# Projecting with the output weights held and h streamed: a GFNet mixing and SwiGLU kernel on one core

## The chip, the core and the metric

The kernel runs on one core of a Trainium2 chip. The metric is device time in microseconds (us) of one execution. TensorE (PE) multiplies matrices and loads the stationary operand with a separate instruction (PEld in the profile); VectorE (DVE), ScalarE (ACT) and GpSimd (POOL) work on elements; SyncE (SP) does no arithmetic here, it issues DMAs. SP and ACT issue DMAs on hardware queues (q1 and q10 in the profile), POOL on a software queue (q0). All queues are served by the same 16 DMA engines. Each engine works through its own instructions in order.

## The reference

`x` has 8 sequences of 3008 tokens with 256 channels, all float32. The first half is a filter in the frequency domain along the sequence, the second half a gated feed-forward layer with 1536 hidden units:

```python
X = np.fft.rfft(x, axis=1)
F = (filt_r + 1j * filt_i)[None, :, :]
y = np.fft.irfft(X * F, n=x.shape[1], axis=1)
g = y @ w_gate
silu = g * (1.0 / (1.0 + np.exp(-g)))
out = (silu * (y @ w_val)) @ w_out
```

## The kernel before

The transform is done by matmuls in stages ("pa", "pb", "pc", "pd" in the profile). The last stage, `stage3`, leaves the mixed tokens transposed, channels on partitions, in a tile `y` of eight parts (L774 to L791).

The feed-forward layer runs over 8 batches, 4 chunks each (752 tokens: two halves i of TH = 376 columns) and 3 groups g of hidden units, so 96 steps; batch 0 goes through its first three chunks group by group and parks partial outputs in `o_dram`. A step has 26 small matrix products (L860; tokens PQABE of the list below) which together give the hidden activations h of its group, as in a fast (Karatsuba- and Strassen-like) scheme with fewer products. ACT and DVE form sums in PSUM and SBUF between them. h stands in two tiles of seven parts, 128 x 376 each; POOL forms four of the combined parts (tokens S).

The projection follows one step later. It is a Strassen-Winograd form with seven products W1 to W7 per step (L932 to L943). Each takes two blocks of hidden units (`JB` = 2) and three windows of 128 tokens, `TOK = (0, 128, 248)`. For each window h is the stationary operand (128 x 128) and 128 columns of `wo_t` are streamed. Three windows of 128 cover 376 tokens, so eight are computed twice. A float32 matmul appears as two MATMUL records in the profile, so a W is 12 records. Results stand tokens on partitions, channels along the row, and after each product an "o" token adds the PSUM bank into the output tile in SBUF (L944 to L952; a copy by ACT for the first one of a chunk).

Stores: tokens x0.o to x5.o (L920 to L931) write the two output tiles `o0`, `o1`, three windows each, from POOL's queue: one DMA per window, 128 rows of 1 KB, six per chunk and only after its last group.

The order of all engines' work is written out by hand in `SCHEDULE` (L88): one step's tokens in order, where a prime means "of the step before last" (the projection's late part), and "t" tokens advance the transform of the next batch. `pin` keeps every engine's instructions in that order. `LAST` (L99) is what is left after the final step. The 26 weight tiles of a group do not fit twice: they are reloaded in place in four pieces (`PIECES`, L407, on SP), each as soon as its last product of the step is done, so that a piece issued after Q2 must be there when the next step opens with Q0.

Of the kernel before, what the change touches and what calls it, by code (L numbers as in the profile page):

```python
# [41 lines left out]
FP32 = mybir.dt.float32  # L42
# [6 lines left out]
B, S, C = 8, 3008, 256  # L49
# [6 lines left out]
NR = 2 * N1  # L56
NK = 4 * NS

NH = 4
NW = 2 * NH  # L60
NCHUNK = 32 // NW
TH = NH * NR
TOK = (0, 128, TH - 128)
NT = 3
NG = 3
JB = NJ // NG
# [11 lines left out]
WO = {1: 0, 7: 1, 2: 2, 3: 3, 5: 4, 6: 5, 4: 6}  # L78
HID = {1: 0, 6: 6, 4: 2, 2: 3, 5: 4, 7: 1, 3: 5}
# [6 lines left out]


SCHEDULE = """  # L88
Q0 o3' t4.2' W2 f0 S00' S01' x0.o' t0.0 x1.o' Q1 t0.1 x2.o' P3 x3.o' f1 t4.3' W1 x4.o' S10' x03 S11'
s13 x5.o' P1 o1 t0.2 P0 o2 c1 D01 A13 g1 c0 S20' Q2 S21' g0 y01 m13 t1.0 h0 f2 s01 W6 t1.1 h1 x23  # L90
D02 P2 o6 D12 A01 c2 B13 g2 n3' m01 t0.3 S30' t1.2 x02 W7 S31' g13 y12 y02 B01 h13 o7 t1.3 t2.0 s02
s12 g01 h2 Q3 t2.1 h01 e12 A02 y23 W4 e02 y03 m02 g3 A12 o4 t2.2 E12 m12 B02 t2.3 l12 E02 u12 e13
g02 t3.0 h3 s23 l02 B12 v12 E13 t3.1 h02 u02 A23 n2 l13 g12 v02 W5 s03 e23 h12 e01 m23 A03 o5 u13
E23 t3.2 m03 v13 E01 l23 e03 t3.3 t4.0 l01 u23 B23 v23 u01 t4.1 E03 n1 v01 g23 B03 l03 W3 h23 g03
u03 h03 v03
""".split()
KS = (-1, 0, 1, 2)

LAST = """  # L99
S00 S01 S10 S11 W1 o1 W2 o2 S20 S21 S30 S31 W6 o6 W5 o5 W3 o3 x0.o x1.o x2.o W7 o7 W4 o4 x3.o x4.o  # L100
x5.o
""".split()
BLOCKS = (0, 1, 3, 2)
PAIRS = ((0, 1), (1, 2), (2, 3), (0, 2), (1, 3), (0, 3))
# [68 lines left out]
def kernel(  # L173
# [10 lines left out]
    nc = tc.nc  # L184
# [18 lines left out]
    wdpool = pool("wdram", 1, DRAM)  # L203
# [24 lines left out]
                  for i in range(4)]  # L228
    yt_dram = [wdpool.tile([128, 3 * len(PAIRS), TQ], FP32, name=f"yt_{k}") for k in range(NT)]
    y_dram = [wdpool.tile([128, 8, TQ], FP32, name=f"y_{k}") for k in range(NCHUNK)]  # L230
    o_dram = [wdpool.tile([2, 128, len(TOK), C], FP32, name=f"o_{k}") for k in range(NT)]
    w_dram = wdpool.tile([NG, 128, NPR, 2, 128], FP32, name="w_all")
    wo_t = cpool.tile([128, NJ, 7, 128], FP32)

# [18 lines left out]
    pin = tc.keep_in_program_order  # L253

    def add(eng, dst, a, b):
        return eng.tensor_tensor(out=dst, in0=a, in1=b, op=ALU.add)  # L256
# [246 lines left out]
    def bank(name):  # L503
        return wps.tile([128, 512], FP32, name=f"w{name}", tag="w")
# [10 lines left out]
    class Spectral:  # L515
# [231 lines left out]
        def stage3(self, k, step):  # L747

            if step == 0:
                self.y[k] = ypool.tile([128, 8, TQ], FP32, name=f"y_{self.b}_{k}", tag="y")  # L750
            i, cb = divmod(step, 2)
            ps = (self.bank if k == 0 else fbank)(f"pd_{self.b}_{k}_{step}")
            psv = ps.rearrange("p a b -> p (a b)")[:, 0:TH].rearrange("p (n r) -> p n r", n=NH)
            flat = ps.rearrange("p a b -> p (a b)")
            back = self.b
            for j in range(len(BACK) if back else 0):
                first = BACK_AT[j]
                cols = back_t[0][:, first:first + N1 * len(BACK[j])]

                if j == 1:  # L760
                    rows = flat[:, 1:2 * 187 + 1].rearrange("p (z y) -> p z y", z=2)[:, :, ::2]
                else:
                    at = j // 2 * (2 * N1 + 1)
                    rows = flat[:, at:at + 6 * N1 - 1:2]
                pin(nc.tensor.matmul(out=rows, lhsT=self.t4[k, i][:, j, ts(cb, 128)], rhs=cols,  # L765
                                     start=j == 0, stop=True, skip_group_check=True))
            for n in range(0 if back else NH):
                pin(nc.tensor.matmul(out=psv[:, n, :],  # L768
                                             lhsT=self.t4[k, i][0:NK, n, ts(cb, 128)],
                                             rhs=wi_t, start=n == 0, stop=True,  # L770
                                             skip_group_check=True))
            yield

            y = self.y[k]  # L774

            def tokens(part, parts):
                return y[:, part:part + parts].rearrange("p t (r n) -> p n (t r)", n=NH)

            if cb == 0:
                pin(nc.scalar.copy(out=tokens(2 * i, 2), in_=psv))  # L780
                return
            for t in range(2):
                a, c = 2 * i + t, psv[:, :, ts(t, N1)]
                b, v, k = tokens(a, 1), tokens(4 + a, 1), KS[a]
                if k == 0:
                    pin(nc.scalar.copy(out=v, in_=c))
                elif k == -1:
                    pin(add(nc.vector, v, c, b))
                else:
                    pin(nc.vector.scalar_tensor_tensor(  # L790
                        out=v, in0=b, scalar=-float(k), in1=c, op0=ALU.mult, op1=ALU.add))  # L791
# [22 lines left out]
    outs = {}  # L814

    def takes_turns(b, k):
        return b == 0 and k < NT

    def new_outs(b, k, g):
        outs[b, k] = [opool.tile([128, len(TOK), C], FP32, name=f"o{i}_{b}_{k}_{g}",  # L820
                                 tag=f"o{i}", bufs=2) for i in range(2)]
        if g:
            for i in range(2):
                pin(nc.sync.dma_start(out=outs[b, k][i], in_=o_dram[k][i]))

    class Group:

# [19 lines left out]
        def bank(self, key, n=2):  # L847
            t = bank(f"{key}_{self.name}")
            self.tiles[key] = t[:, 0:2 * TQ].rearrange("p (z n) -> p z n", z=2) if n == 2 else \
                t[:, 0:384].rearrange("p (t c) -> p t c", c=128)  # L850
            return self.tiles[key]

        def product(self, p, key, start):
# [9 lines left out]
        def step(self, op, eng=None):  # L863
# [48 lines left out]
            elif kind == "n":  # L912
                if self.following:
                    self.following(i)

        def project(self, op, last=False):

            b, k, q = self.b, self.k, self.g
            kind, p = op[0], int(op[1])
            if kind == "x":  # L920
                i, t = divmod(p, len(TOK))
                if q < NG - 1 and takes_turns(b, k) and t == len(TOK) - 1:
                    pin(nc.sync.dma_start(out=o_dram[k][i], in_=outs[b, k][i]))
                if q == NG - 1:
                    skip = TOK[1] + 128 - TOK[2] if t == 2 else 0
                    rows = out[b * S:(b + 1) * S].rearrange("(r n) c -> r n c", n=32)
                    queue = (nc.sync, nc.scalar)[(p + i) % 2] if last else nc.gpsimd
                    pin(queue.dma_start(
                        out=rows[(TOK[t] + skip) // NH:(TOK[t] + 128) // NH, ts(2 * k + i, NH), :],
                        in_=outs[b, k][i][skip:128, t, :]))  # L930
                return  # L931
            at = {1: "A", 6: "A", 7: "A", 4: "A", 2: "F", 5: "G", 3: "G"}[p]  # L932
            if kind == "W":
                start = p in (1, 2, 5)
                if start:
                    self.bank(at, 3)
                for t, t0 in enumerate(TOK):
                    for i in range(JB):
                        pin(nc.tensor.matmul(  # L939
                            out=self.tiles[at][:, t, :], lhsT=self.hs[i][:, HID[p], t0:t0 + 128],  # L940
                            rhs=wo_t[:, JB * q + i, WO[p], :], start=start and t == 0 and i == 0,
                            stop=True, skip_group_check=True))
                return  # L943
            if q == 0 and p == 1:  # L944
                new_outs(b, k, q)
            i, cb = {1: (0, 0), 2: (0, 0), 6: (0, 1), 3: (0, 1), 4: (1, 0), 7: (1, 1),
                     5: (1, 1)}[p]
            dst = outs[b, k][i][:, :, ts(cb, 128)]
            if q == 0 and at == "A":
                pin(nc.scalar.copy(out=dst, in_=self.tiles[at]))  # L950
            else:
                pin(add(nc.vector, dst, dst, self.tiles[at]))  # L952

# [6 lines left out]
    x0 = [t[0:NR, 8 * C * i:8 * C * i + 8 * C] for t, i in ((wo_f, 0), (wo_f, 1), (y_f, 0))]  # L960
    x0 = [t.rearrange("p (n c) -> p n c", c=C) for t in x0]
# [6 lines left out]
    with tc.tile_pool(name="start", bufs=1) as spool0:  # L968
# [3 lines left out]
        f0 = spool0.tile([128, NS, C], FP32, name="f0")  # L972
# [8 lines left out]
        n = 0  # L981
# [68 lines left out]
        for p in ("A13", "A01"):  # L1050
            at = SLOT[p]
# [25 lines left out]
    opool = pool("op", 1)  # L1077
# [57 lines left out]
    for b in range(B):  # L1135
# [36 lines left out]
        for step in range(NCHUNK * NG + (b == B - 1)):  # L1172
            ghost = step == NCHUNK * NG
            k, g = order_of(b)[min(step, NCHUNK * NG - 1)]
# [13 lines left out]
            last = ghost or b == B - 1 and step == NCHUNK * NG - 1  # L1188
            for place, token in enumerate(SCHEDULE):
# [5 lines left out]
                if op[0] == "t":  # L1195
                    n = int(op[1])
# [64 lines left out]
```

## Time and profile before

| what | value |
|---|---|
| median of 7 runs | 2924.79 us (2922.44 to 2929.59) |
| the profiled execution's own time | 2922.45 us |
| its span in the profile | 2920.7 us |
| PE busy | 2887.8 us (99%) |
| DVE busy | 2031.3 us (70%) |
| ACT busy | 1599.7 us (55%) |
| POOL busy | 1595.3 us (55%) |
| granted TensorE clock | 0.998 |

The span is the time from the first to the last instruction; the profiled execution's own time is 1.75 us longer. "Busy" of PE counts overlapping matmuls once and says nothing of how fast they go, so the pace has to be taken from where one run of matmuls starts and the next one starts.

### The profile page before, as it was taken

How to read it: one execution, taken by the hardware profiler on the slowest of the kernel's cores; microseconds unless marked ns; L12 is line 12 of the kernel's file. 1: busy time of each engine (PE TensorE's matmuls, PEld its weight loads, DVE VectorE, ACT ScalarE, POOL GpSimd, SP SyncE). 2: the span in 40 equal slices, each digit the busy share in tenths (PEclk: the TensorE clock that was granted, in tenths of full speed). 3: DMA queues.
4: the chain of work that ended last, by engine and by line, in shares of the span. 5: the costliest groups of instructions: out<-in, count | busy, mean ns of one | idle time of the engine just before them, and what ended most of it. 6: DMA issues, size and time to landing. Idle time of an engine off the chain costs nothing.

```text
span 2920.7 us, 57842 instructions
## 1 busy us (share of the span) xinstructions
PE 2887.8 (99%) x20160; PEld 2830.7 (97%) x20160; DVE 2031.3 (70%) x4536; ACT 1599.7 (55%) x4190; POOL 1595.3 (55%) x1767
## 2 busy tenths in 40 slices
PE   8999999999999999999999999999999999999999
PEld 6889999999999999999999999999999999999999
DVE  6888766676676676767767667676666766666665
ACT  6775455545555555555455555555555555555554
POOL 4876655556454655455554556454565555555453
PEclk9999999999999999999999999999999999999999
DMA  8687865575565655656656566556565566644432
GB/s 229 211 261 249 301 195 188 175 228 180 181 193 181 223 182 175 198 174 211 207 165 203 175 199 213 172 185 194 191 206 179 175 204 196 206 134 159 145 129 88
DMA packets 234325, 559.55 MB, mean 192 GB/s; under 512 B 31757, under 2 KB 128015, under 8 KB 234035
## 3 DMA queue, kind: packets, MB, share of 16 engines
q1 hardware_dynamic: 199169, 486.24, 52.2%
q10 hardware_dynamic: 25938, 45.72, 4.6%
q0 software_dynamic: 8928, 23.89, 2.3%
q8 instruction: 162, 2.65, 0.4%
q14 instruction: 128, 1.05, 0.1%
HBM read 460.38 MB, written 95.34 MB: 190 GB/s over the span
## 4 chain that ended last, share of the span: by engine, by line
PE 93%; DMA 2%; DVE 1%; POOL 1%; issue 0%; SPq 0%; ACT 0%; DVEq 0%; POOLq 0%
PE wa L860 24%; PE wA L939 17%; PE wk L860 16%; PE we L860 12%; PE wG L939 8%; PE wF L939 4%; PE pd L765 3%; PE pc L731 2%; PE pb L698 2%; PE pa L639 1%; PE pa L641 1%; DMA lent<-later_tbl 1%; DMA lent<-d 0%; PE pa L658 0%; PE pd L768 0%
## 5 line engine op out<-in xcount | busy, mean ns | idle before, releaser
L860 PE MATMUL wa<-y_t,wt_t 128*128 128x188 f32 x4464 | 878.8, 323 | 3.8 <-issue 1.4
L860 PEld LDWEIGHTS wa<-y_t,wt_t 128*128 128x128 f32 x4464 | 729.7, 190 | 11.4 <-issue 3.8
L256 POOL TENSOR_TENSOR h<-h 128x376 f32<-128x376 f32 x190 | 182.9, 984 | 766.0 <-DVE h L907 766.0
L939 PE MATMUL wA<-wo_t,h 128*128 128x128 f32 x4608 | 576.9, 275 | 2.6 <-DVE o L256 2.1
L939 PEld LDWEIGHTS wA<-wo_t,h 128*128 128x128 f32 x4608 | 563.0, 192 | 8.6 <-DVE o L256 1.8
L860 PE MATMUL wk<-y,wt_t 128*128 128x188 f32 x2976 | 566.2, 323 | 0.0
L259 POOL TENSOR_TENSOR h<-h 128x376 f32<-128x376 f32 x570 | 562.8, 1009 | 0.5
L860 PEld LDWEIGHTS wk<-y,wt_t 128*128 128x128 f32 x2976 | 479.2, 190 | 7.1 <-DVE y L256 0.6
L860 PE MATMUL we<-y_t,wt_t 128*128 128x188 f32 x2232 | 431.5, 323 | 1.4 <-ACT we L891 1.4
L259 DVE TENSOR_TENSOR we<-we,m 128x376 f32<-128x376 f32 x576 | 317.0, 555 | 161.2 <-PE we L860 110.2
L860 PEld LDWEIGHTS we<-y_t,wt_t 128*128 128x128 f32 x2232 | 369.4, 190 | 1.8 <-ACT we L891 1.7
L259 POOL TENSOR_TENSOR D<-f,f 128x376 f32<-128x376 f32 x288 | 281.5, 991 | 93.8 <-ACT f L875 92.6
L263 DVE SCALAR_TENSOR_TENSOR y<-wk,c 128x376 f32<-128x376 f32 x480 | 244.7, 542 | 107.8 <-ACT we L891 52.1
L895 ACT COPY m<-wa 128x376 f32<-128x376 f32 x576 | 271.8, 472 | 85.2 <-PE wa L860 84.1
L939 PE MATMUL wG<-wo_t,h 128*128 128x128 f32 x2304 | 288.3, 275 | 0.6 <-DVE o L256 0.6
L902 ACT ACTIVATE u<-we 128x188 f32<-128x188 f32 x576 | 188.9, 328 | 179.5 <-DVE we L259 161.2
L902 ACT ACTIVATE g<-wa 128x188 f32<-128x188 f32 x576 | 187.3, 326 | 173.9 <-PE wa L860 166.4
L939 PEld LDWEIGHTS wG<-wo_t,h 128*128 128x128 f32 x2304 | 281.4, 192 | 0.8 <-DVE o L256 0.8
L875 ACT ACTIVATE f<-wk 128x376 f32<-128x376 f32 x288 | 139.3, 484 | 230.6 <-PE wk L860 221.2
L879 ACT COPY c<-wk 128x376 f32<-128x376 f32 x288 | 136.0, 472 | 224.9 <-PE wk L860 224.9
L882 DVE SCALAR_TENSOR_TENSOR x<-wk,f 128x376 f32<-128x376 f32 x192 | 104.3, 543 | 218.4 <-PE wk L860 216.7
L891 ACT COPY we<-y 128x376 f32<-128x376 f32 x480 | 224.3, 486 | 36.0 <-DVE h L907 16.6
(155 smaller groups left out, 4033.8 us busy)
## 6 DMA issues: line engine op xcount, KB each, us to landing
wt_t<-w_all SPq DMA_DIRECT2D x174, 896.0 KB
wt_t<-w_all SPq DMA_DIRECT2D x174, 768.0 KB
lent<-later_tbl SPq DMA_DIRECT2D x84, 256.0 KB
lent<-in_filt_r_dram SPq DMA_DIRECT2D x336, 64.0 KB
d<-lent ACTq DMA_DIRECT2D x84, 256.0 KB
d<-t ACTq DMA_DIRECT2D x78, 240.0 KB
lent<-d SPq DMA_DIRECT2D x144, 128.0 KB
out_dram<-o POOLq DMA_DIRECT2D x124, 128.0 KB, 2.4
```

The source lines that it names most:

```text
L256: return eng.tensor_tensor(out=dst, in0=a, in1=b, op=ALU.add)
L259: return eng.tensor_tensor(out=dst, in0=a, in1=b, op=ALU.subtract)
L263: return nc.vector.scalar_tensor_tensor(out=dst, in0=a, scalar=-1.0, in1=b, op0=ALU.mult, op1=ALU.subtract)
L765: pin(nc.tensor.matmul(out=rows, lhsT=self.t4[k, i][:, j, ts(cb, 128)], rhs=cols, start=j == 0, stop=True, skip_group_check=True))
L860: pin(nc.tensor.matmul(out=ps[:, z], lhsT=self.wt[:, SLOT[p], z], rhs=rhs, start=start and z == 0, stop=True, skip_group_check=True))
L875: pin(act.mul(self.small(f"f{i}", f"f{i}", 1), t[f"k{i}"], -1.0))
L879: pin(act.copy(out=self.small(f"c{i}", f"c{i}", 1), in_=t[f"k{i}"]))
L882: pin(v.scalar_tensor_tensor(out=dst, in0=t[f"k{j}"], scalar=-1.0, in1=t[f"f{i}" if j == 3 else f"D{at}"], op0=ALU.mult, op1=ALU.add))
L891: pin(act.copy(out=self.bank(f"e{at}"), in_=t[f"y{at}"]))
L895: pin(act.copy(out=self.small(f"m{at}", "m", 4), in_=t[f"a{at}"]))
L902: pin(act.activation(out=self.small(op, "g", 3, 1)[:, 0], in_=ps[:, 1], func=AF.Silu))
L939: pin(nc.tensor.matmul(out=self.tiles[at][:, t, :], lhsT=self.hs[i][:, HID[p], t0:t0 + 128], rhs=wo_t[:, JB * q + i, WO[p], :], start=star ...
```

## The change

The operands of the projection change places. The output weights become the stationary operand and h is streamed, 376 columns at once, so a W is two matmuls (four records) in place of six (twelve records). Results then stand channels on partitions and tokens along the row.

To let a chunk's tokens be 32 apart in memory in one row, `stage3` writes `y` with r innermost (n r) in place of n innermost (r n). The two output tiles become one, `[128, 16, 96]`: 16 rows (half i, n, channel half z) of 94 tokens and two spare columns, which POOL sets to zero. New tokens z0 to z3 let VectorE transpose the tile in place in blocks of 32 x 32, one quarter (4 rows of 96) per token; all this only after the last group. The stores read the transposed tile: 12 DMAs per chunk (6 tokens x, two DMAs each), each 32 or 30 partitions x 16 runs of 32 floats (128 bytes). They are issued on SP, at the end alternately on SP and ACT; POOL issues none. In `LAST` all six x tokens stand at the end. The partial outputs of batch 0 go to and from `o_dram` as one DMA each, in runs of 94 floats.

```diff
-x5.o
+S00 S01 S10 S11 W1 o1 W2 o2 z0.o S20 S21 S30 S31 W6 o6 W5 o5 W3 o3 z1.o W7 o7 z3.o W4 o4 z2.o x0.o
+x1.o x2.o x3.o x4.o x5.o
...
-    o_dram = [wdpool.tile([2, 128, len(TOK), C], FP32, name=f"o_{k}") for k in range(NT)]
+    o_dram = [wdpool.tile([128, 4 * NH, NR], FP32, name=f"o_{k}") for k in range(NT)]
...
-                return y[:, part:part + parts].rearrange("p t (r n) -> p n (t r)", n=NH)
+                return y[:, part:part + parts].rearrange("p t (n r) -> p n t r", n=NH)
...
-        outs[b, k] = [opool.tile([128, len(TOK), C], FP32, name=f"o{i}_{b}_{k}_{g}",
-                                 tag=f"o{i}", bufs=2) for i in range(2)]
+        outs[b, k] = opool.tile([128, 4 * NH, RP], FP32, name=f"o_{b}_{k}_{g}", tag="o", bufs=2)
+        if g == NG - 1 or not takes_turns(b, k):
+            pin(nc.gpsimd.memset(outs[b, k][:, :, NR:], 0.0))
...
+            if kind == "z":
+                if q == NG - 1:
+                    t = self.part(p)
+                    pin(nc.vector.transpose(out=t, in_=t))
+                return
...
-                    queue = (nc.sync, nc.scalar)[(p + i) % 2] if last else nc.gpsimd
-                    pin(queue.dma_start(
-                        out=rows[(TOK[t] + skip) // NH:(TOK[t] + 128) // NH, ts(2 * k + i, NH), :],
-                        in_=outs[b, k][i][skip:128, t, :]))
+                    for n, (u, cq) in enumerate(divmod(m, 4) for m in (2 * p, 2 * p + 1)):
+                        rows = min(32, NR - 32 * u)
+                        at = (b * S + 32 * 32 * u + 2 * NH * k) * C + 32 * cq
+                        pin(((nc.sync, nc.scalar)[n] if last else nc.sync).dma_start(
+                            out=bass.AP(tensor=out.tensor, offset=out.offset + at,
+                                        ap=[[32 * C, rows], [128, 4 * NH], [1, 32]]),
+                            in_=t[32 * cq:32 * cq + rows, :, ts(u, 32)]))
...
-                for t, t0 in enumerate(TOK):
-                    for i in range(JB):
-                        pin(nc.tensor.matmul(
-                            out=self.tiles[at][:, t, :], lhsT=self.hs[i][:, HID[p], t0:t0 + 128],
-                            rhs=wo_t[:, JB * q + i, WO[p], :], start=start and t == 0 and i == 0,
-                            stop=True, skip_group_check=True))
+                for i in range(JB):
+                    pin(nc.tensor.matmul(
+                        out=self.tiles[at], lhsT=wo_t[:, JB * q + i, WO[p], :],
+                        rhs=self.hs[i][:, HID[p]], start=start and i == 0,
+                        stop=True, skip_group_check=True))
...
-            dst = outs[b, k][i][:, :, ts(cb, 128)]
+            dst = self.part(2 * i + cb)[:, :, 0:NR].rearrange("p n (t r) -> p t n r", t=2)
+            src = self.tiles[at].rearrange("p (t n r) -> p t n r", t=2, n=NH)
```

In `SCHEDULE` the tokens z1.o', z0.o, z2.o and z3.o are put right behind o3', o2, o4 and o5; no other token moves. z1.o' and the stores x0.o' to x5.o' stand in the first third of a step.

More of the change, by code (lines that the diff above doesn't have):

```diff
@@ L62 @@
 TH = NH * NR
-TOK = (0, 128, TH - 128)
+RP = 96
 NT = 3
@@ L88 @@
 SCHEDULE = """
-Q0 o3' t4.2' W2 f0 S00' S01' x0.o' t0.0 x1.o' Q1 t0.1 x2.o' P3 x3.o' f1 t4.3' W1 x4.o' S10' x03 S11'
-s13 x5.o' P1 o1 t0.2 P0 o2 c1 D01 A13 g1 c0 S20' Q2 S21' g0 y01 m13 t1.0 h0 f2 s01 W6 t1.1 h1 x23
+Q0 o3' z1.o' t4.2' W2 f0 S00' S01' x0.o' t0.0 x1.o' Q1 t0.1 x2.o' P3 x3.o' f1 t4.3' W1 x4.o' S10' x03 S11'
+s13 x5.o' P1 o1 t0.2 P0 o2 z0.o c1 D01 A13 g1 c0 S20' Q2 S21' g0 y01 m13 t1.0 h0 f2 s01 W6 t1.1 h1 x23
 D02 P2 o6 D12 A01 c2 B13 g2 n3' m01 t0.3 S30' t1.2 x02 W7 S31' g13 y12 y02 B01 h13 o7 t1.3 t2.0 s02
-s12 g01 h2 Q3 t2.1 h01 e12 A02 y23 W4 e02 y03 m02 g3 A12 o4 t2.2 E12 m12 B02 t2.3 l12 E02 u12 e13
-g02 t3.0 h3 s23 l02 B12 v12 E13 t3.1 h02 u02 A23 n2 l13 g12 v02 W5 s03 e23 h12 e01 m23 A03 o5 u13
-E23 t3.2 m03 v13 E01 l23 e03 t3.3 t4.0 l01 u23 B23 v23 u01 t4.1 E03 n1 v01 g23 B03 l03 W3 h23 g03
+s12 g01 h2 Q3 t2.1 h01 e12 A02 y23 W4 e02 y03 m02 g3 A12 o4 z2.o t2.2 E12 m12 B02 t2.3 l12 E02 u12 e13
+g02 t3.0 h3 s23 l02 B12 v12 E13 t3.1 h02 u02 A23 n2 l13 g12 v02 W5 s03 e23 h12 e01 m23 A03 o5
+z3.o u13 E23 t3.2 m03 v13 E01 l23 e03 t3.3 t4.0 l01 u23 B23 v23 u01 t4.1 E03 n1 v01 g23 B03 l03 W3 h23 g03
 u03 h03 v03
@@ L99 @@
 LAST = """
-S00 S01 S10 S11 W1 o1 W2 o2 S20 S21 S30 S31 W6 o6 W5 o5 W3 o3 x0.o x1.o x2.o W7 o7 W4 o4 x3.o x4.o
-x5.o
+S00 S01 S10 S11 W1 o1 W2 o2 z0.o S20 S21 S30 S31 W6 o6 W5 o5 W3 o3 z1.o W7 o7 z3.o W4 o4 z2.o x0.o
+x1.o x2.o x3.o x4.o x5.o
 """.split()
@@ L776, in tokens @@
             def tokens(part, parts):
-                return y[:, part:part + parts].rearrange("p t (r n) -> p n (t r)", n=NH)
+                return y[:, part:part + parts].rearrange("p t (n r) -> p n t r", n=NH)
             if cb == 0:
-                pin(nc.scalar.copy(out=tokens(2 * i, 2), in_=psv))
+                pin(nc.scalar.copy(out=tokens(2 * i, 2),
+                                   in_=psv.rearrange("p n (t r) -> p n t r", t=2)))
                 return
@@ L783, in stage3 @@
                 a, c = 2 * i + t, psv[:, :, ts(t, N1)]
-                b, v, k = tokens(a, 1), tokens(4 + a, 1), KS[a]
+                b, v = [y[:, part].rearrange("p (n r) -> p n r", n=NH) for part in (a, 4 + a)]
+                k = KS[a]
                 if k == 0:
@@ L819, in new_outs @@
     def new_outs(b, k, g):
-        outs[b, k] = [opool.tile([128, len(TOK), C], FP32, name=f"o{i}_{b}_{k}_{g}",
-                                 tag=f"o{i}", bufs=2) for i in range(2)]
+        outs[b, k] = opool.tile([128, 4 * NH, RP], FP32, name=f"o_{b}_{k}_{g}", tag="o", bufs=2)
+        if g == NG - 1 or not takes_turns(b, k):
+            pin(nc.gpsimd.memset(outs[b, k][:, :, NR:], 0.0))
         if g:
-            for i in range(2):
-                pin(nc.sync.dma_start(out=outs[b, k][i], in_=o_dram[k][i]))
+            pin(nc.sync.dma_start(out=outs[b, k][:, :, 0:NR], in_=o_dram[k]))
     class Group:
@@ L849, in bank @@
             self.tiles[key] = t[:, 0:2 * TQ].rearrange("p (z n) -> p z n", z=2) if n == 2 else \
-                t[:, 0:384].rearrange("p (t c) -> p t c", c=128)
+                t[:, 0:TH]
             return self.tiles[key]
@@ L914, in step, with part @@
                     self.following(i)
+        def part(self, p):
+            i, cb = divmod(p, 2)
+            return outs[self.b, self.k].rearrange("p (i n z) r -> p i z n r", i=2, z=2)[:, i, cb]
         def project(self, op, last=False):
@@ L919, in project @@
             kind, p = op[0], int(op[1])
+            if kind == "z":
[3 more added lines that the diff above has]
+                return
             if kind == "x":
-                i, t = divmod(p, len(TOK))
-                if q < NG - 1 and takes_turns(b, k) and t == len(TOK) - 1:
-                    pin(nc.sync.dma_start(out=o_dram[k][i], in_=outs[b, k][i]))
+                t = outs[b, k]
+                if q < NG - 1 and takes_turns(b, k) and p == 5:
+                    pin(nc.sync.dma_start(out=o_dram[k], in_=t[:, :, 0:NR]))
                 if q == NG - 1:
-                    skip = TOK[1] + 128 - TOK[2] if t == 2 else 0
-                    rows = out[b * S:(b + 1) * S].rearrange("(r n) c -> r n c", n=32)
-                    queue = (nc.sync, nc.scalar)[(p + i) % 2] if last else nc.gpsimd
-                    pin(queue.dma_start(
-                        out=rows[(TOK[t] + skip) // NH:(TOK[t] + 128) // NH, ts(2 * k + i, NH), :],
-                        in_=outs[b, k][i][skip:128, t, :]))
+                    for n, (u, cq) in enumerate(divmod(m, 4) for m in (2 * p, 2 * p + 1)):
[5 more added lines that the diff above has]
+                            in_=t[32 * cq:32 * cq + rows, :, ts(u, 32)]))
                 return
@@ L947, in project @@
                      5: (1, 1)}[p]
-            dst = outs[b, k][i][:, :, ts(cb, 128)]
+            dst = self.part(2 * i + cb)[:, :, 0:NR].rearrange("p n (t r) -> p t n r", t=2)
+            src = self.tiles[at].rearrange("p (t n r) -> p t n r", t=2, n=NH)
             if q == 0 and at == "A":
-                pin(nc.scalar.copy(out=dst, in_=self.tiles[at]))
+                pin(nc.scalar.copy(out=dst, in_=src))
             else:
-                pin(add(nc.vector, dst, dst, self.tiles[at]))
+                pin(add(nc.vector, dst, dst, src))
     rpool = pool("raw", 1)
```

## The prediction

> **What bounds the kernel now.** First the page: busy shares, slices, DMA queues and the chain that ended last.
>
> ```profile
> PE 2887.8 (99%) x20160; PEld 2830.7 (97%) x20160; DVE 2031.3 (70%) x4536; ACT 1599.7 (55%) x4190; POOL 1595.3 (55%) x1767
> DMA  8687865575565655656656566556565566644432
> q1 hardware_dynamic: 199169, 486.24, 52.2%
> q10 hardware_dynamic: 25938, 45.72, 4.6%
> q0 software_dynamic: 8928, 23.89, 2.3%
> PE 93%; DMA 2%; DVE 1%; POOL 1%; issue 0%; SPq 0%; ACT 0%; DVEq 0%; POOLq 0%
> ```
>
> The chain is TensorE's for 93%. Then the busy time by stretch, to see where TensorE is not the bound (first column: length; then PE busy):
>
> ```profile
> 0.00:350.00 350.00, 323.87 (x2071) 293.90 (x2072) 277.31 (x587) 224.09 (x574) 226.31 (x293) 0.99 0.79 247
> 1000.00:2000.00 1000.00, 1000.00 (x7026) 988.27 (x7025) 688.52 (x1541) 539.64 (x1411) 534.03 (x575) 1.00 0.59 190
> ```
>
> From 350 us on TensorE never stops; all its idle time lies in the start and the last 20 us. So in 93 steps of 96 the time is the sum of TensorE's paces. The timeline of TensorE gives these: start of a run, start of the next run, divided by the count.
>
> ```profile
> 134.85 1.02 PE L658 MATMUL pa<-x,wf_t 94*96 94x512 f32 x2
> 135.71 0.80 PE L860 MATMUL wa<-y_t,wt_t 128*128 128x188 f32 x4
> ...
> 1000.07 1.03 PE L731 MATMUL pc<-lent 128*128 128x256 f32 x4
> 1000.93 0.80 PE L860 MATMUL wa<-y_t,wt_t 128*128 128x188 f32 x4
> 1001.57 0.80 PE L860 MATMUL we<-y_t,wt_t 128*128 128x188 f32 x4
> ...
> 1002.84 1.50 PE L939 MATMUL wG<-wo_t,h 128*128 128x128 f32 x12
> 1004.18 0.80 PE L860 MATMUL wa<-y_t,wt_t 128*128 128x188 f32 x4
> ```
>
> 512 columns pace at 0.86/2 = 0.430 us, 256 at 0.86/4 = 0.215, 188 at 0.64/4 = 0.160, 128 at 1.34/12 = 0.112. That is 0.84 ns a column at 256 and 512, and 0.87 at 128.
>
> **TensorE's part.** A W now takes 12 x 0.112 = 1.34 us. After: 4 records of 376 columns. Between the rows of 256 and 512: 376 x 0.84 = 0.316, so 1.264 us; from the row of 188 doubled: 0.320, so 1.28 us. Two effects, eight columns fewer in 384 and no short-matmul loss. Saved per W 0.060 to 0.076; with 7 x 96 = 672 W's 40 to 51 us. I take 50: 376 lies between 256 and 512. All of it is on the path where TensorE never stops.
>
> **VectorE's part.** Added: 4 transposes x 32 chunks = 128 of 384 elements. No transpose is in this trace. From below: an operation on 376 elements, whose starts follow each other by 0.47 us (1548.93 and 1549.40 below). From above: the dearest SBUF add, `x_third`, 1190 ns for 256 elements, so 1.8 us for 384. I take 0.5, because the common rows all go by about one element per ns. 128 x 0.5 = 64 us on an engine with 30% idle. What each delays can be read from VectorE's timeline at a step's start (idle time in brackets):
>
> ```profile
> 1544.74 0.55 DVE L256 TENSOR_TENSOR o<-o,wG 128x384 f32<-128x384 f32 x1 [0.31 <-PE wG L939]
> 1548.93 0.55 DVE L882 SCALAR_TENSOR_TENSOR x<-wk,f 128x376 f32<-128x376 f32 x1 [3.63 <-PE wk L860]
> 1549.40 0.55 DVE L882 SCALAR_TENSOR_TENSOR wa<-wk,f 128x376 f32<-128x376 f32 x1
> ...
> 1552.79 0.54 DVE L256 TENSOR_TENSOR o<-o,wF 128x384 f32<-128x384 f32 x1
> 1553.97 0.54 DVE L882 SCALAR_TENSOR_TENSOR wa<-wk,D 128x376 f32<-128x376 f32 x1
> 1556.32 0.55 DVE L882 SCALAR_TENSOR_TENSOR x<-wk,D 128x376 f32<-128x376 f32 x1 [1.10 <-ACT g L902]
> ```
>
> z1 falls into the 3.63 us of idle behind o3 and costs nothing. z0 comes behind o2 (1552.79), ahead of the sum `wa` that ends at 1554.51 and that TensorE takes up with A01 at about 1555.33: 0.8 us of slack, and 1.10 us of idle behind; 0.5 goes in. Behind o5 this step shows idle gaps of 0.46 and 0.84 us within 4 us, behind o4 1.80. I charge 0.1 us per chunk, 3 us. If the cover is gone, all four lie on the path: 2 us per chunk, 64 us. The output adds go from 384 to 376 elements in runs of 47: 0.55 us by the row of `we` (555 ns), at worst 0.99 by the 494 ns for 188 strided elements of L790; I take 0.55.
>
> **Stage 3's new layout.** ACT's 62 copies of 848 ns (L780) should fall to the 472 ns of a plain 376 copy, 23 us in all; the 188-element forms from about 500 to 345 ns. All beside TensorE, nobody waits on them now: 0.
>
> **POOL.** 186 issues of 579 ns go (107 us), 35 small memsets come; the dearest comparable row is 0.5 us for 128 columns, 17 us. POOL already waits 766 us for h: 0, cover is that wait.
>
> **Stores.** Runs per chunk: 4 x (32 + 32 + 30) x 16 = 6016, on 16 engines 376 each; 32 chunks make 12,032 packets per engine. No store of 128 bytes is in this trace. The trace's packet records have medians of 22 ns for 376 bytes, 27 for 512 and 46 for 1024. From below by bytes, 46/8: 6 ns. From above the mean q10 packet, 4.6% x 16 x 2920.7 / 25,938 = 83 ns (1763 bytes). I take 22 ns, the nearest record. Then 265 us per engine, 9.1% of the span, in place of q0's 2.3%: the DMA share goes from 59.6% to 66%. From 6 to 83 ns it is 60 to 91%.
>
> The Trainium skill speaks against this change: "DMA: Bandwidth & Descriptors", section Specifications, says that a transfer under 512 bytes makes the DMA engine read, modify and write. By that rule, as an estimate with the 27 ns for 512 bytes taken twice, a run would cost 54 ns, 20 us per chunk and engine. No packet of this trace is a store so short, so the rule is neither confirmed nor refuted by it.
>
> What stands behind the stores on SP's queue decides. Its timeline at the same step:
>
> ```profile
> 1547.15 2.06 SPq L530 DMA_DIRECT2D x<-in_x_dram  x3
> 1552.74 0.35 SPq L407 DMA_DIRECT2D wt_t<-w_all  x1
> 1559.20 2.19 SPq L530 DMA_DIRECT2D x<-in_x_dram  x3
> ```
>
> The stores can start when z1 ends, 1544.74 + 0.55 + 0.5 = 1545.8. Twelve issues of 0.76 us (median of the four `out_dram` issues that SP makes today) and the x loads end at 1557, so the reload of the first weight piece goes out 4 us later than 1552.74. At 213 GB/s (that stretch) its 896 KB land 4.3 us on, at 1561.5. The next step's Q0 starts at 1574.7: 13 us to spare, cost 0. The x loads are three units ahead of use. With 378 more issues SP works 861 + 287 us of 2920.
>
> **Batch 0.** Twelve transfers of partial outputs now run in 376-byte pieces, 128 packets per engine, 2.8 us each; the DMA share there is 0.79. I charge 1 us.
>
> **Slack.** Where TensorE now arrives 0.075 us earlier at a sum that ACT or VectorE still owes, part of the gain is lost. All sums are in time today; I charge 2 us.
>
> **The end.** Timeline of the last 5 us:
>
> ```profile
> 2912.79 5.14 SPq L928 DMA_DIRECT2D out_dram<-o  x4
> 2915.80 0.56 DVE L256 TENSOR_TENSOR o<-o,wA 128x384 f32<-128x384 f32 x1 [1.70 <-PE wA L939]
> ```
>
> From the end of that add (2916.36) to the span's end it takes 4.3 us with one or two issues per queue left. After: z2 0.5, z0 0.5 (VectorE sets the pace there), six issues per queue at 0.76 in place of one or two, +3.5. Together +4.5; if packets cost 83 ns, 384 x 83 = 32 us, up to +28.
>
> **Sum.** 2922.45 - 50 + 3 + 1 + 2 + 4.5 = 2883 for the profiled execution, which lies 2.3 us below the median; so 2885 to 2886 against the median. I say 2886, 1.3% faster. A measurement of this kernel tells about 0.2% (6 us) from no change.
>
> **Rivals.**
> 1. Slower: the stores hold the ring and the weight reload comes late. Place: behind x5.o', piece Q2. From 1545.8 to 1574.7 there are 28.9 us; less 4.3 for the reload and 3 for the x loads leaves 21.6 us for 376 packets: it decides from 57 ns. At 70 ns the packets take 26.3 us, 4.7 late, 32 x 4.7 = 150: 3036; at 83 ns 9.6 late, 3193. For it: no row under 376 bytes. Against it: records rise evenly with size (22, 27, 46 ns). Chance 0.15.
> 2. Slower: transposes at 1.8 us, or adds at 0.99, make VectorE late. Cover is about 1 us each and more for z1, so 0.8 x 3 = 2.4 us per chunk, 77 us: 2960. Decides from about 1.4 us a transpose. Chance 0.06.
> 3. The matmuls shorten, but the loop through ACT and VectorE at a step's end (E03, its subtraction, Silu, product, then W2) sets the step for part of them: half the gain, 2908. For it: the order is tuned to today's paces. Against: TensorE waits nowhere. Chance 0.14.
> 4. The change does not do what it says: a record of 376 paces like three of 128 (0.335). Then 4 x 0.335 = 1.34, no gain, plus 10 of added costs: about 2934. Chance 0.05.
>
> **How the numbers follow.** Forecast 0.60 (2872 to 2898), rivals as above. Faster by over 0.2%: 0.60 + 0.14 = 0.74. Within 0.2%: 0.04, edges of rivals 3 and 4. Slower: 0.22. The range: the whole 51 us without any cost is 2874, so from 2872; up to 2970 it takes in rivals 3, 4 and 2, about 0.83.
>
> **What would show it.** Records of L951, 128x376, four to a W, at 0.316; TensorE still without a stop from 350 us on; no PE wait on `o`, `wt_t` or DMA; transposes near 0.5 us; q0 gone, q1 up by 192,512 packets at about 22 ns; the reload after Q2 issued some 4 us later in one step of three. I am wrong if the 128-byte packets take over 57 ns, if a transpose takes over 1.4 us, or if TensorE shows waits for VectorE spread over the steps.

## The result, and the profile after

The changed kernel takes 2916.76 us (median of 15 runs, 2910.98 to 2919.78), the kernel before 2924.65 us beside it (35 runs). The ratio is 0.9972 with a 95% interval of 0.9965 to 0.9979: 8 us faster, where 39 were forecast. The profiled execution took 2918.89 us, its span is 2917.1 us, 3.6 us shorter than before's. These two executions lie 2.1 us above and 2.2 us below their medians, so the traces account for some 4 us of gain and the medians for 8.

Page of the changed kernel: PE's share (first line), the DMA share in 40 slices, the two hardware queues, the chain that ended last.

```profile
PE 2849.3 (98%) x14784; PEld 2440.9 (84%) x14784; DVE 2074.9 (71%) x4664; ACT 1576.1 (54%) x4190; POOL 1496.4 (51%) x1613
DMA  8799865666665666566556676565665666645443
q1 hardware_dynamic: 415349, 509.81, 58.5%
q10 hardware_dynamic: 28752, 45.85, 4.7%
PE 90%; DMA 2%; DVE 1%; POOL 1%; issue 0%; ACT 0%; SPq 0%; DVEq 0%; POOLq 0%
```

PE is idle 68 us of the span (2917.1 less 2849.3); before, it was 33. The chain, still PE's, gives it 90% in place of 93%. Something stops TensorE for some 35 us that did not before, and the page does not say where. The windows do (first column the length, then the busy time of PE, PEld, DVE, ACT, POOL; at the end the granted clock, the DMA share and GB/s). The changed kernel:

```profile
200.00:350.00 150.00, 139.26 (x670) 112.77 (x669) 116.31 (x249) 78.26 (x209) 86.22 (x105) 0.99 0.94 244
350.00:500.00 150.00, 128.65 (x630) 110.59 (x629) 90.41 (x202) 64.21 (x175) 65.93 (x68) 0.92 0.61 187
1000.00:2000.00 1000.00, 999.12 (x5215) 863.74 (x5213) 718.89 (x1619) 537.92 (x1430) 509.80 (x527) 1.00 0.63 194
```

The kernel before, same view:

```profile
200.00:350.00 150.00, 147.70 (x989) 139.68 (x988) 121.64 (x262) 83.08 (x224) 90.32 (x109) 1.00 0.82 272
350.00:500.00 150.00, 150.00 (x1059) 148.31 (x1057) 103.32 (x234) 82.43 (x217) 85.56 (x95) 1.00 0.62 204
```

Between 200 and 500 us TensorE is idle 32.1 us in place of 2.3, and in the second half of that stretch the granted clock is 0.92 in place of 1.00. Between 200 and 350 us the DMA engines are busier (0.94 against 0.82) and move less (244 against 272 GB/s). Later nothing of the kind: 999.12 us of 1000.

A second reading puts a price on each place: the start of each step (its first gate and value product on TensorE's timeline), after less before.

| step | 4 | 8 | 9 | 10 | 11 | 12 | 95 |
|---|---|---|---|---|---|---|---|
| start before, us | 203.7 | 326.5 | 357.5 | 387.8 | 417.2 | 446.3 | 2877.9 |
| after less before, us | -3.1 | +1.9 | +17.7 | +21.8 | +21.7 | +33.8 | -6.6 |

From step 12 to step 95 the changed kernel gains 40.4 us, 0.49 a step. Between steps 4 and 12, all in batch 0, it loses 36.9. From the start of step 95 to the end of the span it loses 3.0 more (-6.6 to -3.6).

What TensorE waits for in that stretch, 200 to 500 us, changed kernel (total us, times, longest):

```profile
PE pb L698 <- DMA lent<-d: 13.6, 4, 8.8
PE pd L765 <- DMA t<-d: 9.5, 1, 9.5
PE pb L698 <- issue: 5.0, 2, 2.7
PE pa L658 <- DMA x<-in_x_dram: 1.6, 1, 1.6
```

All of them belong to the transform of batch 1, which runs inside batch 0's steps, and the large ones are loads. SP issues these loads, and now it issues the stores too. Its timeline in step 8 (start, time, instruction), changed kernel:

```profile
337.39 10.76 SPq L940 DMA_DIRECT2D out_dram<-o  x12
348.24 0.42 SPq L495 DMA_DIRECT2D paired<-paired_tbl  x1
...
352.37 0.43 SPq L530 DMA_DIRECT2D lent<-later_tbl  x1
352.84 2.16 SPq L530 DMA_DIRECT2D lent<-in_filt_r_dram  x4
355.10 1.29 SPq L530 DMA_DIRECT2D lent<-in_filt_i_dram  x2
358.39 0.39 SPq L530 DMA_DIRECT2D lent<-d  x1
```

The kernel before, the same group of loads:

```profile
335.34 0.45 SPq L530 DMA_DIRECT2D lent<-later_tbl  x1
335.90 3.11 SPq L530 DMA_DIRECT2D lent<-in_filt_r_dram  x4
340.88 2.62 SPq L530 DMA_DIRECT2D lent<-in_filt_i_dram  x2
344.08 0.39 SPq L530 DMA_DIRECT2D lent<-d  x1
```

`lent<-d`, which `pb` waits for, is issued at 358.39 in place of 344.08, 14.3 us later, of which 1.9 are the later start of step 8. Twelve stores stand ahead of it for 10.76 us, 0.9 us each. So the first theory: in batch 0 the stores delay batch 1's loads by the order of SP's queue. The rival: the spill of partial outputs, now in pieces of 376 bytes, fills the DMA engines. A third possibility is that both do.

The interval of an experiment below is mostly 0.14 to 0.18% to either side, 4 to 5 us. Smaller differences between two experiments are read from their traces, one execution each, and are that much weaker.

### The profile page after: what moved, and what is told of

It reads as the page before. It is cut to its first block, busy times and chain, and to the rows that moved or that the text cites. A ratio compares the mean times of both kernels' runs of the same rounds, so it can differ in the third digit from the quotient of the medians.

```text
span 2917.1 us, 47274 instructions
## 1 busy us (share of the span) xinstructions
PE 2849.3 (98%) x14784; PEld 2440.9 (84%) x14784; DVE 2074.9 (71%) x4664; ACT 1576.1 (54%) x4190; POOL 1496.4 (51%) x1613
## 4 chain that ended last, share of the span: by engine, by line
PE 90%; DMA 2%; DVE 1%; POOL 1%; issue 0%; ACT 0%; SPq 0%; DVEq 0%; POOLq 0%
PE wa L862 24%; PE wA L951 16%; PE wk L862 16%; PE we L862 12%; PE wG L951 8%; PE wF L951 4%; PE pd L765 3%; PE pc L731 3%; PE pb L698 2%; PE pa L639 1%; PE pa L641 1%; DMA lent<-later_tbl 1%; DMA x<-in_x_dram 0%; DMA lent<-d 0%; DVE o L256 0%
## 5 line engine op out<-in xcount | busy, mean ns | idle before, releaser
L862 PEld LDWEIGHTS wa<-y_t,wt_t 128*128 128x128 f32 x4464 | 750.8, 190 | 85.3 <-ACT wa L888 9.1
L862 PEld LDWEIGHTS wk<-y,wt_t 128*128 128x128 f32 x2976 | 502.8, 190 | 80.4 <-issue 0.8
L951 PE MATMUL wA<-h,wo_t 128*128 128x376 f32 x1536 | 550.1, 481 | 2.0 <-DVE o L256 1.3
L951 PEld LDWEIGHTS wA<-h,wo_t 128*128 128x128 f32 x1536 | 280.9, 190 | 106.2 <-DVE o L256 2.8
L951 PE MATMUL wG<-h,wo_t 128*128 128x376 f32 x768 | 274.3, 479 | 1.2 <-DVE o L256 1.2
L909 DVE TENSOR_TENSOR h<-wa,g 128x188 f32<-128x188 f32 x576 | 197.0, 346 | 32.9 <-ACT g L904 32.0
```

The costliest lines, as they stand in the source:

```text
L862: pin(nc.tensor.matmul(out=ps[:, z], lhsT=self.wt[:, SLOT[p], z], rhs=rhs, start=start and z == 0, stop=True, skip_group_check=True))
L909: pin(v.tensor_tensor(out=dst, in0=ps[:, 0], in1=g, op=ALU.mult))
L951: pin(nc.tensor.matmul(out=self.tiles[at], lhsT=wo_t[:, JB * q + i, WO[p], :], rhs=self.hs[i][:, HID[p]], start=start and i == 0, stop=Tru ...
```

## Experiments: which of the two loads batch 0

**Batch 0's stores from POOL's queue (e1).**

```diff
-                        pin(((nc.sync, nc.scalar)[n] if last else nc.sync).dma_start(
+                        pin(((nc.sync, nc.scalar)[n] if last else nc.gpsimd if b == 0 else nc.sync).dma_start(
```

> The changed kernel, with the stores of batch 0 alone issued on POOL's queue instead of SP's; nothing else moves. Queue theory: in batch 0 the 12 store issues of chunks 0 to 2 stand on SP in front of the loads of batch 1's second transform stage, and TensorE waits for those loads. Then the losses of +15.8, +4.1 and +12.1 us that the starts of steps 9, 10 and 12 show go: 2917 - 30 = about 2887 us, and TensorE's wait of 8.8 us for lent<-d is gone. Rival, short pieces: the 376-byte pieces of the partial outputs fill the DMA engines in batch 0. They stay here, so the time stays at 2912 to 2917.

Measured 2910.68 us, ratio to before 0.9946 (0.9930 to 0.9963). Step 8 starts +8.3, step 12 +23.4, step 95 -14.1 us against before. That is just under what the rival expected and far from the theory: 6 us come back. One part of the theory did come true: the longest wait for `lent<-d` between 200 and 500 us fell from 8.8 to 2.0 us. But the time went to other waits (POOL's h 3.6, `y_t` 3.1), and steps 8 to 12 still lose 15.1 us.

**The spill in whole rows (e2).** The DRAM tile gets the two spare columns, so each partition is written as 6144 contiguous bytes instead of 16 pieces of 376; the stores stay on SP.

```diff
-    o_dram = [wdpool.tile([128, 4 * NH, NR], FP32, name=f"o_{k}") for k in range(NT)]
+    o_dram = [wdpool.tile([128, 4 * NH, RP], FP32, name=f"o_{k}") for k in range(NT)]
...
-        if g == NG - 1 or not takes_turns(b, k):
+        if g == 0:
...
-            pin(nc.sync.dma_start(out=outs[b, k][:, :, 0:NR], in_=o_dram[k]))
+            pin(nc.sync.dma_start(out=outs[b, k], in_=o_dram[k]))
...
-                    pin(nc.sync.dma_start(out=o_dram[k], in_=t[:, :, 0:NR]))
+                    pin(nc.sync.dma_start(out=o_dram[k], in_=t))
```

> The changed kernel, with the partial outputs of batch 0 kept and fetched as whole tiles, 6144 bytes per partition in one piece (with the two spare columns, zeroed at the first group). Stores stay on SP. Rival, short pieces: most of the 37.6 us lost in batch 0 comes back, about 2885. Queue theory: only the small losses of steps 4 to 8 (1.3, 1.7 and 2.0 us) come back, 2911 to 2914; the waits of 8.8 us for lent<-d and 9.5 for t<-d stay.

Measured 2907.0 us, 0.9934 (0.9919 to 0.9949): 10 us come back. Step 8 now starts at -5.0, step 12 still at +21.4. The DMA queues between 200 and 350 us (packets, MB, share of the 16 engines), changed kernel and then e2:

```profile
q1 hardware_dynamic: 37340, 33.33, 87.2%
```

```profile
q1 hardware_dynamic: 22196, 34.58, 72.9%
```

More bytes in 14 points less of the engines' time. Up to step 8 the spill explains the loss: the changed kernel and e1, which keep it, lose 5.0 us (-3.1 to +1.9) and 10.5 us (-2.2 to +8.3) from step 4 to step 8; e2, which writes whole rows, loses nothing there (-3.6 to -5.0). The first two do the same work up to there, since batch 0's first store is in step 8, so the 5.5 us between them show how far two executions can differ. From step 8 on the waits of e2 (200 to 500 us) are the ones seen before:

```profile
PE pb L698 <- DMA lent<-d: 9.7, 3, 8.7
PE pd L765 <- DMA t<-d: 8.6, 1, 8.6
```

**Both (e3).** The edits of e1 and e2 together.

> Both edits: batch 0's stores on POOL, partial outputs as whole rows. Either theory: the steady gain of 0.49 us per step from the first step on, 96 x 0.49 = 47, less 3.5 us for the longer end and 1 of start: 2925 - 43 = 2882 us. If it stays above 2895, something else in batch 0 is lost, the added packets or the transposes.

Measured 2897.74 us, 0.9901 (0.9886 to 0.9915). The two edits brought 6.1 and 9.8 us alone and bring 19.0 together, so both causes are real, and by these medians each partly hides behind the other. It is not the 2882 hoped for: steps 8 to 12 still lose 11.8 us (-2.4 to +9.4). But what TensorE waits for between 200 and 500 us has changed:

```profile
PE wa L862 <- DVE wa L884: 5.6, 4, 1.4
PE wA L951 <- POOL h L259: 4.5, 4, 1.8
...
PE pb L698 <- DMA lent<-d: 0.7, 2, 0.4
```

The loads are on time, and results of POOL (h) and of VectorE come late instead. Groups of POOL between 330 and 430 us, e3 (count, busy us, mean ns):

```profile
L940 POOL DMA_DIRECT2D out_dram<-o x30 | 20.0, 671 | 0.0
L259 POOL TENSOR_TENSOR h<-h 128x376 f32<-128x376 f32 x20 | 19.3, 987 | 0.0
```

Thirty stores of 671 ns stand among the sums of h and D that POOL owes the other engines: the cure appears to have a price of its own, and e8 below shows that these waits go when the stores do.

**The kernel before with its stores on SP (e4)** asks whether the place of the stores matters without any other part of the change. Six stores of 128 KB a chunk, 1 KB runs.

```diff
-                    queue = (nc.sync, nc.scalar)[(p + i) % 2] if last else nc.gpsimd
+                    queue = (nc.sync, nc.scalar)[(p + i) % 2] if last else nc.sync
```

> The kernel before, with its six stores of 1 KB rows per chunk issued on SP instead of POOL. No transposes, no short pieces. Queue theory: 6 x 0.6 us in front of the same loads in three steps of batch 0 cost 5 to 15 us there, 2930 to 2940; steady steps stay. Rival, short pieces: nothing changes, 2925.

Measured 2929.22 us, 1.0013 (1.0003 to 1.0022): 3.5 us slower than before, little, and below the 2930 to 2940 of the theory. In the trace the mechanism stands alone, though. Steps 8 and 9 start at +0.6 and +5.8, and +5.8 stays unchanged through step 12; SP's timeline and TensorE's only DMA wait between 300 and 400 us, e4:

```profile
334.34 4.47 SPq L928 DMA_DIRECT2D out_dram<-o  x6
```

```profile
PE pb L698 <- DMA lent<-d: 4.4, 1, 4.4
```

Six stores of 4.47 us make the same `pb` wait 4.4 us for the same load. After that the place on SP costs next to nothing (step 95 starts at +6.2).

## Experiments: is anything else lost in batch 0

e3 left 11.8 us between steps 8 and 12. Is that the issuing of stores on whichever engine, the traffic of the stores, or a third cause? All kernels from here to e11 have e2's whole-row spill. In e8 the line that decides whether a store is made differs, in the others only the line that picks the queue.

**No stores in batch 0 (e8).**

```diff
-                if q == NG - 1:
+                if q == NG - 1 and b:
```

> Whole-row spill as in e2, and batch 0's stores are left out: the first 3008 rows of the output are not written. It bounds what these 48 stores can cost on any queue. Theory (the stores' issuing is the rest of the loss): steps 8 to 12 then lose nothing against the kernel before beyond the 0.49 us gained per step: step 12 starts about 4 us earlier than before's, 2883 us in all (2880 to 2887). Rival (something else in batch 0 costs the 11 us that are left in e3): 2893 us or more.

Measured 2882.26 us, 0.9858 (0.9843 to 0.9872). Steps 4, 8 and 12 start at -2.6, -4.1 and -2.7: the loss is all but gone, and step 95 starts at -43.0. This kernel leaves out the first sequence of the output, so it bounds what the stores cost and is no replacement. The windows of e8:

```profile
200.00:350.00 150.00, 144.79 (x711) 118.70 (x710) 123.22 (x265) 83.46 (x223) 88.21 (x105) 1.00 0.79 263
350.00:500.00 150.00, 149.72 (x787) 129.65 (x786) 107.75 (x246) 81.42 (x219) 74.67 (x78) 1.00 0.58 190
```

A third cause of any size is out: steps 8 to 12 still lose 1.4 us where, at 0.49 a step, 2.0 should be gained. Of the 34.5 us between the changed kernel and e8, 9.8 go with the spill's rows and 24.7 with batch 0's 48 stores, their issue and their traffic together; e11 below tells how much a change of queue alone brings back.

**The stores on ACT's queue (e7).**

```diff
-                        pin(((nc.sync, nc.scalar)[n] if last else nc.sync).dma_start(
+                        pin(((nc.sync, nc.scalar)[n] if last else nc.scalar if b == 0 else nc.sync).dma_start(
```

> Whole-row spill as in e2, batch 0's 48 stores on ScalarE's queue instead of SyncE's or GpSimd's. In e3 DMA waits of TensorE are gone between 180 and 480 us, but GpSimd spends 8 us per step on issuing 12 stores (671 ns each) and TensorE then waits 4.0 us for h from GpSimd; step 12 starts 11.8 us later against the kernel before than step 8 does. Theory (the rest of e3's loss is GpSimd's issuing): ScalarE is busy 46 of 100 us there and issues a store in 0.56 us, 6.7 us a step that fit into its idle time; the 11.8 us shrink to 3 or less: 2886 to 2891 us. Rival 1 (the rest is the stores' traffic itself, whoever issues it): 2896 to 2899 us as e3. Rival 2 (ScalarE feeds TensorE directly, so an issue there costs more than on GpSimd): 2899 us or more, with waits of TensorE for ACT between 320 and 460 us.

Measured 2908.37 us, 0.9943 (0.9928 to 0.9957): the second rival's case. Idle time on average does not help an engine whose single results are awaited. ACT's timeline, e7, and TensorE's largest wait between 318 and 470 us:

```profile
322.94 3.88 ACTq L940 DMA_DIRECT2D out_dram<-o  x4
326.92 0.58 ACT L739 COPY lent<-pc 128x512 f32<-128x512 f32 x1 [3.98 <-DMA out_dram<-o]
327.53 0.35 ACTq L745 DMA_DIRECT2D d<-lent  x1
327.92 3.66 ACTq L940 DMA_DIRECT2D out_dram<-o  x4
331.68 0.48 ACT L877 ACTIVATE f<-wk 128x376 f32<-128x376 f32 x1 [4.18 <-DMA d<-lent]
```

```profile
PE wk L862 <- ACT f L877: 13.3, 4, 4.8
```

A store costs ACT 0.7 to 1.0 us here, not the 0.56 of the kernel's end on which the theory went, and four in a row hold `f` back by 4 us.

**Shared between SP and POOL (e9)**, one of every two stores each.

```diff
-                        pin(((nc.sync, nc.scalar)[n] if last else nc.sync).dma_start(
+                        pin(((nc.sync, nc.scalar)[n] if last else (nc.sync, nc.gpsimd)[n] if b == 0 else nc.sync).dma_start(
```

> Whole-row spill as in e2, batch 0's stores half on SyncE's queue and half on GpSimd's. SyncE then has some 5 us of stores a step ahead of batch 1's loads in place of 10, GpSimd 4 us in place of 8. Theory (each queue has a few us of slack a step, so half a block costs less than half): 2890 to 2896 us. Rival (cost in proportion to what each queue issues): half of e2's and half of e3's, 2902 us.

Measured 2891.55 us, 0.9892 (0.9875 to 0.9908), as the theory of a slack on each queue had it. Step 9 starts at +5.4 and step 12 at +5.2: what is left, 9.4 us, is lost in step 8 alone. SP's timeline there, e9:

```profile
329.71 5.03 SPq L940 DMA_DIRECT2D out_dram<-o  x6
...
337.99 8.41 SPq L530 DMA_DIRECT2D lent<-in_filt_r_dram  x4
346.50 0.84 SPq L530 DMA_DIRECT2D lent<-in_filt_i_dram  x2
347.38 0.43 SPq L530 DMA_DIRECT2D lent<-d  x1
```

**Shared between SP, POOL and ACT (e10)**, four of a chunk's twelve each, and **chunk 0's on POOL, the others shared by SP and POOL (e11)**.

```diff
-                        pin(((nc.sync, nc.scalar)[n] if last else nc.sync).dma_start(
+                        pin(((nc.sync, nc.scalar)[n] if last else (nc.sync, nc.gpsimd, nc.scalar)[(2 * p + n) % 3] if b == 0 else nc.sync).dma_start(
```

> Whole-row spill, batch 0's stores shared by three queues (SyncE, GpSimd, ScalarE in turn, four of a chunk's twelve each). In e9 what is left is 9.4 us in step 8, where one wait of 6.3 us for a load of lent stands behind six stores on SyncE (5.03 us) and four loads whose issue took 8.41 us. Theory (each queue's slack is a few us, a third of a block fits into it): 2884 to 2889 us. Rival (the packets in flight slow the loads down, whoever issues them): step 8 keeps its 9 us and the time is that of e9, 2890 to 2894 us; ScalarE's share may add waits of TensorE for f from ACT as in e7 (13.3 us for twelve).

```diff
-                        pin(((nc.sync, nc.scalar)[n] if last else nc.sync).dma_start(
+                        pin(((nc.sync, nc.scalar)[n] if last else (nc.gpsimd if k == 0 else (nc.sync, nc.gpsimd)[n]) if b == 0 else nc.sync).dma_start(
```

> Whole-row spill, chunk 0's stores of batch 0 all on GpSimd (as in e3, which lost 4.5 us in step 8 where e9 lost 9.4), chunks 1 to 3 half and half (as in e9, which lost nothing from step 9 to 12 where e3 lost 7.3). Theory (the places add up, step by step): e9's 2891.5 less 4.9 us, 2887 us (2885 to 2889). Rival (the loads of step 8 pushed back by what GpSimd has late meet the next steps): 2890 us or more.

e10: 2895.88 us, 0.9901 (0.9885 to 0.9918), a miss: no better than e9, near what its rival expected. It loses 11.6 us in step 8 (-2.4 to +9.2), its waits between 318 and 470 us are still `pb <- lent<-d` (7.1 us), and none is for ACT. SP's timeline in step 8, e10:

```profile
332.35 3.17 SPq L940 DMA_DIRECT2D out_dram<-o  x4
335.62 3.08 SPq L495 DMA_DIRECT2D paired<-paired_tbl  x1
...
340.59 9.03 SPq L530 DMA_DIRECT2D lent<-in_filt_r_dram  x4
...
350.60 0.43 SPq L530 DMA_DIRECT2D lent<-d  x1
```

Four stores take 1.9 us less than e9's six, but the load right behind them takes 3.08 us to issue (0.41 in e9) and the four of `lent` 9.03. From the end of the `y_t` load in front of the stores to the issue of `lent<-d` it takes 17.8 us with six stores on SP (e9), 18.4 with four (e10) and 19.9 with twelve (e2), against 14.9 with the stores on ACT (e7), 10.5 with them on POOL (e3, e11) and 11.7 without stores (e8). So it is the stores' place on SP that makes the loads late, but not in proportion to their number, and the 0.9 us per issue is not the whole mechanism. What slows the issue of the loads behind them, no run isolates.

e11: 2887.19 us, 0.9874 (0.9860 to 0.9889), the 2887 that the sum by steps gave. All stores are made here, so 19.8 of the 24.7 us come back by the choice of queue alone. Between steps 4 and 12 it loses 2.9 us, and TensorE has between 350 and 500 us nearly what it had before the change, 149.08 of 150:

```profile
350.00:500.00 150.00, 149.08 (x780) 128.36 (x780) 109.30 (x244) 80.98 (x216) 87.70 (x97) 1.00 0.66 201
```

By its median it is the fastest kernel of this study that writes the whole output: 1.3% under before and 1.0% under the changed kernel.

**Each transpose three times (e5)**, on the changed kernel as it was, asks how much cover VectorE has.

```diff
-                    pin(nc.vector.transpose(out=t, in_=t))
+                    for _ in range(3):
+                        pin(nc.vector.transpose(out=t, in_=t))
```

> The changed kernel with each transpose in place done three times (an odd number, so the output stays): 128 x 2 x 0.578 us = 148 us more work on VectorE, which is busy 71% of the time. Theory (the transposes lie beside TensorE's work, 0.15 us a chunk shows): 2917 to 2927 us, most of it at the end, where the last transpose of the last chunk stands on the path (1.2 us each). Rival (VectorE's order makes them part of the path, two waits of a step hold on them): 1.2 us per transpose, 2917 + 128 x 1.2 = up to 3065 us, at half of that 2990 us.

Measured 2970.75 us, 1.0160 (1.0142 to 1.0178): between the two expectations. 256 more transposes of 578 ns are 148 us of work, and 54 us of it show against the changed kernel, 0.21 us of each 0.578. The waits of e5 between 1000 and 2000 us name where:

```profile
PE pc L731 <- DVE lent L714: 13.8, 9, 2.2
PE wa L862 <- DVE wa L884: 3.2, 5, 0.6
```

The changed kernel has 0.5 us of the first and none of the second there. So one transpose at a time lies beside TensorE's work, and three do not: the cover ends between 0.58 and 1.73 us.

## Why the prediction was right or wrong

**TensorE's part: right.** Timeline of the changed kernel:

```profile
1003.00 0.80 PE L862 MATMUL wa<-y_t,wt_t 128*128 128x188 f32 x4
1003.63 1.43 PE L951 MATMUL wG<-h,wo_t 128*128 128x376 f32 x4
1004.89 0.80 PE L862 MATMUL wk<-y,wt_t 128*128 128x188 f32 x4
```

From 1003.63 to 1004.89 is 1.26 us for four records, 0.315 each, as interpolated from the rows of 256 and 512 columns. Seven W's a step at 0.076 saved are 0.53 us; 0.49 a step were gained from step 12 to 95. Rival 4 (no gain in pace) is out, and so is rival 3 (the loop at a step's end): TensorE is busy 999 of 1000 us at the new pace.

**The transposes: right, a little too cheap.** Group of VectorE, changed kernel:

```profile
L930 DVE STREAM_TRANSPOSE o<-o 128x384 f32<-128x384 f32 x128 | 74.0, 578 | 4.4
```

578 ns against 0.5 us assumed, far from the 1.4 at which rival 2 was to decide; e5 shows what a dear transpose would have cost: at 3 x 0.578 = 1.73 us, 54 / 32 = 1.7 us a chunk, where rival 2 had 2.4 at 1.8. The output adds take 543 to 546 ns (0.55 assumed). The slack (2 us) and z (3 us) together: TensorE should have gained 0.53 x 83 = 44 from step 12 to 95 and gained 40.4, so 3.6 were lost. POOL (99 us less busy) and ACT (24 us less) changed nothing in the steady steps, as charged.

**Stores in the steady steps: right, with the price on the wrong row.** A 128-byte packet takes 12 ns (median of 189,504 on q1), not 22, and the DMA share went to 63.6%, not 66. TensorE shows no wait for `wt_t` or `x` from 500 us on, so rival 1, which needed 57 ns, is out. The Trainium skill ("DMA: Bandwidth & Descriptors", section Specifications) has DMA engines read, modify and write for anything under 512 bytes; the estimate made from it, 54 ns, is not met by these stores.

**The end: right.** +4.5 charged, 3.0 lost between the start of step 95 and the end of the span. The last lines of VectorE's timeline, changed kernel:

```profile
2908.82 0.55 DVE L256 TENSOR_TENSOR o<-o,wA 128x376 f32<-128x376 f32 x1 [1.01 <-PE wA L951]
2909.41 0.58 DVE L930 STREAM_TRANSPOSE o<-o 128x384 f32<-128x384 f32 x1
```

The last transpose ends at 2909.99, and 7.1 us of stores follow.

**Batch 0: wrong, and it is the whole miss.** The step that failed is "Twelve transfers of partial outputs now run in 376-byte pieces, 128 packets per engine, 2.8 us each; the DMA share there is 0.79. I charge 1 us." Steps 4 to 12 lost 36.9 us. Two things are wrong in it:

1. The size. 22 ns for 376 bytes is right for the reads of the spill (22 to 24 ns mean in the trace's packet records) but not for its writes: 50 to 63 ns mean, 32 median, for the four writes between 200 and 316 us. At 58 ns, 128 packets are 7.4 us per engine. The last packets of these four writes ended 9.5 to 11.0 us after issue; in whole rows (e2) 4.3 to 5.6. Worth 9.8 us by e2, at a DMA share that was 0.79 already. Here the rule quoted above and the record go the same way; whether reading and writing back is why these writes are dear, no run shows.
2. What was left out. "What stands behind the stores on SP's queue decides" is the right question, but it was answered from one timeline, at 1547 us, where a weight piece with "13 us to spare, cost 0" stands behind them. In batch 0 SP also issues eight loads for every unit of batch 1's stage 2, a unit every 12 us (335.34 and 347.70 in before's timeline), and TensorE takes them up within the step. Before's SP timeline from 330 to 350 us shows it. Worth 24.7 us by e8, of which e11 gets 19.8 back with all stores made.

Without this term the sum stands: e8, which takes both causes away, measures 2882.26 against 2885 (2886 less the 1 us), though it also leaves out 48 of the 384 stores. None of the three signs of being wrong that the prediction named came up (packets 12 ns, transposes 0.58 us, waits for VectorE of 1.0 us in all from 500 us on); what failed was its sign of being right, that TensorE does not stop from 350 us on. The sign of the forecast was right; 2916.76 lies outside its likeliest case (2872 to 2898), and no rival named this mechanism: rival 1 had the right queue, but the wrong transfer behind the stores.

## What to carry to other kernels

When a step is moved to another queue, read that queue's timeline in every phase of the program, start-up and hand-over included, not at one steady step: the same twelve stores made TensorE wait for no load in 28 chunks and cost some 20 us in the first four. Then ask who waits for what is queued behind them, because an idle engine is no free place either: on ACT the same stores made TensorE wait for `f`, on POOL for h, and sharing them between SP and POOL (2891.55 us) was better than giving them all to either (2907.0 and 2897.74). When a tile gets a pad, let the parking place in DRAM have it too, so that its rows stay whole.

## What the runs showed of the hardware that was not expected

- A packet's price is not a function of its size alone. Stores of 128 bytes took 12 ns; the six spill writes in pieces of 376 bytes took 45 to 63 ns on average, spill reads in the same pieces 22 to 24.
- Issuing these stores is dear on every queue: 0.48 us median on SP over the whole run (315 to 3302 ns), 0.8 to 0.9 us in step 8 on SP, 0.7 to 1.0 us there on ACT, 0.67 us on POOL. Loads behind them can be slow to issue too: four of `lent` took 8.41 us behind six stores in e9 and 9.03 behind four in e10, but 2.16 behind twelve in the changed kernel.
- A lower granted clock goes with long idle stretches: 0.92 between 350 and 500 us in the changed kernel, 1.00 in e11, where TensorE is not kept waiting. Of the 36.9 us lost, 29.8 are idle time. The clock is the next part: in the changed kernel's trace it is 0.50 for 27.3 us between 340 and 457 us, and there four records of 188 columns take 1.26 us (starts at 363.87 and 365.13) in place of 0.64. TensorE works 18.3 of these 27.3 us, so about 9 us are lost to it. Idle time and clock, less the 4 us that 8 steps should gain, make 35 of the 36.9 us.
- VectorE's transpose in 32 x 32 blocks of 384 float32 columns takes 578 ns, about the time of an add on as many elements (0.55).
